# A delta-rule attention feeding an MLP on one core: small identity products at the head of TensorE's program, and another order of the prologue

## The chip, the cores and the metric

The kernel runs on one core of a Trainium2 chip. The metric is the device time of one execution in microseconds (us). A core has engines that run side by side, each with its own program, in order: TensorE (PE in the profile, its weight loads PEld), VectorE (DVE), ScalarE (ACT), GpSimd (POOL) and SyncE (SP), which here only issues DMA transfers. An instruction that needs another engine's result waits on a semaphore, and everything behind it on its engine waits with it.

## The reference

Four batches, eight heads, 768 tokens, head dimension 48. For each head the state is a 48 x 48 matrix that is updated token by token; the outputs, laid out as 3072 tokens x 384, go through an MLP with hard-swish.

```python
k_n = k / (np.linalg.norm(k, axis=-1, keepdims=True) + 1e-06)
for t in range(S):
    y[:, :, t] = np.einsum('bhd,bhde->bhe', q[:, :, t], state)
    v_old = np.einsum('bhde,bhd->bhe', state, kt)
    state = state + bt[:, :, :, None] * np.einsum('bhd,bhe->bhde', kt, vt - v_old)
...
h = x @ w_in                       # 3072 x 384 by 384 x 2048
g = h * np.clip(h + 3.0, 0.0, 6.0) / 6.0
return (g @ w_out).astype(np.float32)
```

All inputs and outputs are float32.

## The kernel before

**The tiling.** Tokens are taken in 24 steps (t = 0 to 23) of 32 tokens; four batches of 32 tokens fill the 128 partitions. Inside a step the token-by-token recurrence is turned into products of 32 x 32 matrices per head and batch, with the inverse of a triangular matrix; between steps the 48 x 48 states are carried. Two steps make one block of 256 tokens for the MLP.

**One step of attention** has these parts, each a generator that gives its work out in pieces:

- `norms` (L397 to L434): the key norms, a square on ScalarE (L407), a sum and four small rows on VectorE (L413 to L431), a root on ScalarE (L417).
- `prep` (L505): normalised keys `kb` on POOL (L510), transposes of keys and queries on TensorE (pt, L524), their copies KQ on ScalarE (L532), the scores sc on TensorE (L547, 32 small products for a step), and two masked copies on VectorE (L558), called L and LB.
- `mask` (L475) and `scaled` (L494) on POOL: the masks with beta (L486) that L558 multiplies by, and keys times beta (L498). The mask of step t waits for the L of step t - 2.
- the inverse. Step 0 has its own (`product`, L569: pi at L596). Steps 1 to 4 form a group: `halves_of` (L715) turns their four L into one tile A on VectorE (L469), eliminates with 14 pairs of rows `pr` and `A` (L730, L735), and turns it back into X (L473). For each of these steps `join` (L666) then makes the whole inverse from two halves: a transpose on VectorE (L694), 32 products pi1 (L684), a sum and a transpose (L698, L702), 32 products pi2, and a copy into X on ScalarE (L710).
- `chain` (L787): products with the state, ks (L806); R on VectorE (L901, L909); pz = X by R (L827) and its copy on ScalarE, also called R (L927); the state's update su on TensorE (L938) and on VectorE (L956); and `output`: y (L843, L819), py (L827), yt (L873) and its copy xT (L877), which is the MLP's input.

**The MLP.** `up` (L982) makes h for a chunk of 128 features as three products ph (L994), then on ScalarE a relu (L1001) and on VectorE g (L1004). `down` (L1153) multiplies by w_out. Later blocks use versions with fewer products (L1059, L1207). Before a weight is used it is converted: weights arrive as 16 pieces of 768 KB that SP loads (L331) into `spare` or into parts of w_out, four rows on ScalarE make a scale (`scales`, L356), and three rows on VectorE (`convert`: L378, L383, L389) make the piece. There are two scale tiles, so the first scale row of piece i waits for L389 of piece i - 2, and `up` of two chunks waits for one piece of w_in.

**The order.** The first 5 steps or so are not scheduled by rule. A string, `ORDER` (L22 to L41), gives one word for each piece of work, and the engines' programs stand in that order: `k`, `q`, `v`, `w` a load; `n`, `p`, `m`, `b`, `x`, `h`, `y` a piece of `norms`, `prep`, `mask`, `scaled`, `product`/`join`, `chain`, `output` of the step that is named; `i1` a piece of the inverse of steps 1 to 4; `a` one scale row, `c` one conversion row, `s` and `z` settings on POOL and VectorE; `ua`, `ra`, `ga` one chunk of `up` for the first half block, its relu and its g. `x2*3` is the word three times. After the string a loop (L1469) runs step by step, with the work spread by budgets.

PSUM tiles come from rings: four buffers for transposes, pi, pz, py, yt and ph, and two pairs of banks for sc, ks and su. A new tile takes the buffer whose reader was issued first.

Of the kernel before, what the change touches and what calls it, by code (L numbers as in the profile page):

```python
# [22 lines left out]
k*2 B*3 k*2 n0 k*2 z B s*2 n0*6 k*2 q*2 n1 q n1 q w k p0 z*3 k n1*2 k*2 n1*2 z p0*2 s k p0*3 a k a  # L23
m0 a n2 m1 p0 x0*2 w q x0 n1 x0*3 c*2 n2 a k s p1*2 a s*2 k q s*2 x0 n2 k*2 c x0 n2 x0 w q a*4 q p1
n2 k*2 a x0 m2 p1 c*2 p1 n2*3 b1 q b0 s p1 x0 q w x0 n2 q*2 c*3 x0 n4 k p1 k p2*2 x0*2 a*2 c a*2 q*3
a*2 w v p3*2 q x0 q n4 p2*2 c p2 v c n4*2 a*3 z v n4 c a m3 v c p2 n4*2 q p2 k c b2 h0 c h0 w a*2 h0
p4*2 a*2 m4 p3 q*4 h0 q k w p4*2 c*5 v*2 p3 k p3*3 k*2 p4*2 v*2 p4 m6 k a w a w i1*3 k i1*7 a i1*2 a
i1*2 v i1*2 k b3 k y0 c y0*3 ua*2 ra*2 i1*3 w v ga v a*3 i1*2 ua i1 h1 i1 q w ua ra ua i1 ra*2 ga i1
k ua a*2 ra ga i1 ga ua ra ua ra i1 ga i1*4 ua ga n5 x1*2 k x1 c a ra v a*2 ga x2 k*2 ga*2 ua*2 x1
ra*2 x1*2 ua h1*2 n5 k ga c ra ga*2 h1 c y1*2 ua ra w ga ua ra x2 n5 ga y1*2 ua ra ga h1 v*3 n5*2 k  # L30
y1*2 ua a ra x2 ub*2 a n5 rb*2 h1 x3 ga c*2 v W a h2 y2 gb ub rb gb x2 gb ub*2 n5*2 b4 rb n5 x2*2 h2
gb rb gb m5 a n5*2 y2 ub rb gb v c q*2 v q*5 n5 ub n5 rb gb h2 c h2 q ub y2 h2 y2 rb ub p5 b5 rb
gb*2 a*2 x3 p5 ub y2*2 k p5*2 h2 rb h3 p5 gb h3 ub*2 q rb gb rb gb ub a x3 p6 v c x4 x3 rb gb ub p7
rb gb y3 c*2 v c p7*2 y3 v p7*2 b6 x3 q x3 ub p6 h3 a p6 c p5*2 rb gb k m7 w p6 h3 u p6 k*2 q*3 a*2
y3 a p6 c y3 v y3*2 u n9 v k q a c a c*2 u*2 ru gu w k a*2 c a*2 x4 c*2 ru p7 a gu k u a*2 p7 p6 m8
u*3 a k u*2 k h3 w ru*2 a*2 gu*2 x4 c*2 x4 k c*2 a p8 k a*2 u ru k h3 u*2 h4 ru a b8 gu k gu y4 p8*3
u h4 k*2 c q k*9 q u p8*2 x4 k ru k*2 gu k c n9 q u q*2 p8 k*2 b7 n9*2 i2 u x4 q i2*2 q ub ru gu u
rb gb i2*2 h4*2 u*2 i2 ru i2*6 y4 i2 gu i2*7 u i2 ru gu i2 u*3 ru i2*4 gu ru i2*2 v i2 c gu u*3 a u
ru c i2 u*2 i2 gu i2*3 q i2*5 y4 h4 n9 i2 e*2 n9*2 i2*4 q i2 y4 e n9 u ru i2*3 u i2 ru*2 gu h4 u n9
i2*2 u i2 e i2*6 y4 u k n9*3 u gu i2 y4 n9 i2 p9 q i2*2 gu  # L40
"""  # L41


# [1 line left out]
def kernel(  # L45
# [21 lines left out]
    nc = tc.nc  # L67
    B, H, S, D = q.shape
    DM, FF = moe_w_in.shape
    C, DP = 32, 64  # L70
# [11 lines left out]
    G0 = 1  # L82
# [12 lines left out]
    def rows(b):  # L95
        return slice(C * b, C * b + C)
# [4 lines left out]
    def group(t):  # L101
        return (0, t) if t < G0 else ((t - G0) // GS + 1, (t - G0) % GS)
# [34 lines left out]
    def needs(*what):  # L137
        assert past.issuperset(what), (what, set(what) - past)
# [70 lines left out]
    ident = const.tile([128, 128], FP32, name="ident")  # L209
# [284 lines left out]
    def scaled(t):  # L494
# [7 lines left out]
        past.add(("bkb", t))  # L502
        yield

    def prep(t, whole=True):  # L505

        g, i = group(t)
# [9 lines left out]
        for j, src in enumerate((kb, qb)):  # L517
            if j == 1:
                needs(("q", t))
                past.add(("qT", t))  # L520
            ring("pm", NPM, ("pt", t, j))
            pt = psM.tile([128, NP, P], FP32, name="pt", tag=slot["pm"])
            for p in range(NP):
                nc.tensor.transpose(  # L524
                    pt[:, p, :], src[:, 2 * p : 2 * p + 2].rearrange("p e w -> p (e w)"), ident[:]
                )
            yield 1
            if j == 0:
                ring("KQ", NKQ, ("KQ", t))
                KQ = work.tile([128, NP * B // 2, 4, C], FP32, name="KQ", bufs=NKQ)  # L530
            read(("pt", t, j))
            nc.scalar.activation(  # L532
                out=KQ[:, :, 0:4:3, :] if j == 0 else KQ[:, :, 1:3, :],
                in_=pt[:].rearrange("q p (x y c) -> q (p x) y c", y=2, c=C), func=ACTF.Copy,
            )
            if whole and j == 0:
                drain(mask(t))
            yield
# [3 lines left out]
        for p in range(NP):  # L542
            for b in range(B):
                for e in range(2):
# [4 lines left out]
                        lhsT=kq[:, 3 if b % 2 else 0, :],  # L549
                        rhs=kq[:, 3:1:-1, :] if b % 2 else kq[:, 0:2, :],  # L550
                        start=True, stop=True,
# [114 lines left out]
    def join(t):  # L666
# [11 lines left out]
        def times(name, m, k):  # L678
            ring("pm", NPM, (name, t))
            ps = psM.tile([P, H, HC], FP32, name="pi", tag=slot["pm"])  # L680
            for h in range(H):
                for b in range(B):
                    r = slice(C * b, C * b + k)
                    nc.tensor.matmul(  # L684
                        ps[rows(b), h, :], lhsT=m[r, h, :], rhs=LT[r, h, HC:C],
                        start=True, stop=True, skip_group_check=True,
                        tile_position=(C * b, C * b),
                    )
            return ps
# [6 lines left out]
        ps = times("pi1", T, HC)  # L696
# [10 lines left out]
        ps = times("pi2", T2, C)  # L707
# [694 lines left out]
    def early_norms(t):  # L1402
# [7 lines left out]
        a=scales(), c=rest, w=pieces(), q=queries(), v=values(), B=betas(), k=keys(), z=settings(), s=more_settings(),  # L1410
        ua=up(0, 0), ub=up(0, 1), u=mlp_units(),
# [40 lines left out]
    with tc.manual_schedule():  # L1452
        for word in ORDER.split():
            word, _, n = word.partition("*")
# [14 lines left out]
        for t in range(LS, N):  # L1469
            g, i = group(t)  # L1470
# [94 lines left out]
```

## Time and profile before

| | |
|---|---|
| runs | 661.84, 663.70, 664.44 us; median 663.7 |
| the profiled execution | 662.06 us, span 660.3 |
| TensorE busy | 632.5 us, 96% of the span, 11640 matmul passes |
| VectorE busy | 499.2 us, 76% |
| ScalarE busy | 282.3 us, 43% |
| POOL busy | 225.1 us, 34% |
| chain that ended last | TensorE 91%, VectorE 3%, DMA 2% |
| DMA | 33.28 MB, of it instructions 1.49 MB in 91 packets (q8) |

In the rows of a timeline the first two numbers are the start from the span's beginning and the duration in us, then engine, line, operation, output tile from input tiles, shape and count; a bracket tells how long the engine stood idle before and what released it. A float32 matmul of the program can be two passes on TensorE, so 32 small products stand as x64. Spans are modelled at a matmul's end. "PEclk" is the granted TensorE clock as a share of full speed.

The profile shows two stretches: a prologue of some 61 us, where TensorE is busy in parts, and then 599 us in which it is busy throughout.

### The profile page before, as it was taken

To read this page: it belongs to the slowest core of one execution; us is meant where nothing else is said; L and a number is where in the kernel's file an instruction comes from. 1 tells how busy PE (TensorE), PEld (TensorE's weight loads), DVE (VectorE), ACT (ScalarE), POOL (GpSimd) and SP (SyncE) were. 2 spreads that over 40 slices of the span, in tenths; PEclk is the share of its full clock that TensorE was granted. 3 is DMA by queue.
4 is the path that set the end of the run, shared out by engine and by line. 5 is a ranking of instruction groups with operands and counts; after the bars stand their busy time and mean duration, and the time that the engine had idled before them with its cause. 6 is when DMAs were issued, how large, how long until landed. Compare 5 with 4: busy or idle time off the path is not lost.

```text
span 660.3 us, 26640 instructions
## 1 busy us (share of the span) xinstructions
PE 632.5 (96%) x11640; PEld 569.2 (86%) x11640; DVE 499.2 (76%) x1170; ACT 282.3 (43%) x548; POOL 225.1 (34%) x352
## 2 busy tenths in 40 slices
PE   2768999999999999999999999999999999999997
PEld 2658987776689989999999999999999999999997
DVE  5899877798657988758988848979658998456354
ACT  5887689332243154154154244244244144153250
POOL 6531022003661353553254354164051242331430
PEclk9998999999999999999999999999999999999999
DMA  7888346202040030041030030020020020000000
GB/s 174 204 198 235 77 102 164 51 25 43 9 87 18 3 74 3 3 90 22 3 74 3 2 74 3 2 63 2 3 50 2 3 49 3 23 18 2 26 1 24
DMA packets 88692, 33.28 MB, mean 50 GB/s; under 512 B 80224, under 2 KB 83424, under 8 KB 88576
## 3 DMA queue, kind: packets, MB, share of 16 engines
q1 hardware_dynamic: 88224, 31.29, 20.8%
q8 instruction: 91, 1.49, 0.9%
q10 hardware_dynamic: 352, 0.30, 0.2%
q14 instruction: 25, 0.20, 0.1%
HBM read 26.84 MB, written 4.72 MB: 48 GB/s over the span
## 4 chain that ended last, share of the span: by engine, by line
PE 91%; DVE 3%; DMA 2%; SPq 1%; ACT 1%; issue 1%; DVEq 0%
PE po L1226 28%; PE ph L1066 27%; PE ph L994 9%; PE po L1162 6%; PE ks L806 4%; PE su L938 3%; PE pt L524 3%; PE pz L827 3%; PE py L827 3%; PE sc L547 2%; PE yt L873 1%; DMA spare<-in_moe_w_in_dram 1%; PE pi L684 1%; DMA w_out<-in_moe_w_in_dram 1%; SPq L168 1%
## 5 line engine op out<-in xcount | busy, mean ns | idle before, releaser
L1066 PE MATMUL ph<-xT,w_in 128*128 128x128 f32 (+1 forms) x720 | 156.8, 321 | 0.0
L1030 POOL TENSOR_TENSOR g<-g 128x256 f32<-128x256 f32 (+1 forms) x144 | 88.6, 616 | 104.7 <-ACT g L1080 99.1
L1066 PEld LDWEIGHTS ph<-xT,w_in 128*128 128x128 f32 x720 | 116.8, 191 | 6.7
L1226 PE MATMUL po<-w_out,g 128*128 128x192 f32 x640 | 110.6, 326 | 0.0
L1226 PEld LDWEIGHTS po<-w_out,g 128*128 128x128 f32 x640 | 104.6, 190 | 0.5
L1080 ACT ACTIVATE g<-ph 128x512 f32<-128x512 f32 x72 | 43.1, 598 | 105.1 <-PE ph L1066 105.1
L1226 PE MATMUL po<-spare,g 128*128 128x192 f32 x480 | 86.7, 332 | 0.0
L1226 PEld LDWEIGHTS po<-spare,g 128*128 128x128 f32 x480 | 77.2, 190 | 1.8
L994 PE MATMUL ph<-xT,w_in 128*128 128x128 f32 (+1 forms) x384 | 72.0, 338 | 0.6 <-ACT xT L877 0.6
L1236 POOL TENSOR_TENSOR o<-o,u 128x192 f32<-128x192 f32 x18 | 13.3, 739 | 163.8 <-ACT o L1233 86.6
L994 PEld LDWEIGHTS ph<-xT,w_in 128*128 128x128 f32 x384 | 59.6, 195 | 7.7 <-ACT xT L877 0.8
L1093 DVE TENSOR_TENSOR g<-ph,g 128x256 f32<-128x256 f32 x72 | 30.2, 419 | 46.8 <-PE ph L1066 33.5
L759 DVE TENSOR_TENSOR pr<-A 128x30 f32<-128x30 f32 (+9 forms) x150 | 57.3, 382 | 3.3
L1212 DVE TENSOR_TENSOR g<-g 128x512 f32<-128x512 f32 x80 | 56.1, 722 | 3.5 <-PE po L1226 3.5
L1113 DVE SCALAR_TENSOR_TENSOR g<-o,g 128x512 f32<-128x512 f32 x72 | 52.6, 730 | 7.8 <-ACT o L1110 7.7
L764 DVE TENSOR_TENSOR A<-A,pr 128x30 f32<-128x30 f32 (+9 forms) x150 | 55.1, 367 | 3.3
L1110 ACT ACTIVATE o<-g,halves 128x512 f32<-128x512 f32 x72 | 52.2, 725 | 11.3 <-DVE g L1113 8.4
L1066 PE MATMUL ph<-beta_tok,sums_in 128*128 128x128 f32 x288 | 55.9, 275 | 0.0
L356 ACT ACTIVATE spare<-spare,places 128x768 uint16<-128x768 uint16 (+1 forms) x56 | 52.8, 947 | 3.2 <-DMA kf<-in_k_dram 1.6
L1233 ACT ACTIVATE o<-po 128x192 f32<-128x192 f32 x40 | 13.3, 332 | 82.7 <-PE po L1226 79.2
L510 POOL TENSOR_TENSOR kb<-kf,inv 128x384 f32<-128x384 f32 x24 | 21.7, 907 | 75.5 <-issue 43.1
L1162 PE MATMUL po<-w_out,g 128*128 128x384 f32 x128 | 45.4, 490 | 0.0
(141 smaller groups left out, 1019.1 us busy)
## 6 DMA issues: line engine op xcount, KB each, us to landing
kf<-in_k_dram SPq DMA_DIRECT2D x96, 48.0 KB, 2.6
qb<-in_q_dram SPq DMA_DIRECT2D x96, 48.0 KB, 2.4
vf<-in_v_dram SPq DMA_DIRECT2D x96, 48.0 KB, 2.1
out_dram<-o SPq DMA_DIRECT2D x90, 48.0 KB, 1.6
spare<-in_moe_w_in_dram SPq DMA_DIRECT2D x4, 768.0 KB, 6.6
w_out<-in_moe_w_in_dram SPq DMA_DIRECT2D x4, 768.0 KB, 6.1
w_out<-in_moe_w_out_dram SPq DMA_DIRECT2D x4, 768.0 KB, 5.8
spare<-in_moe_w_out_dram SPq DMA_DIRECT2D x4, 768.0 KB, 5.2
```

Source lines behind the costliest of these rows:

```text
L356: nc.scalar.activation(out=z, in_=z if n else d.bitcast(I16)[:, :, :, 3], func=func, bias=places[:, n : n + 1], scale=scale,)
L759: nc.vector.tensor_tensor(out=pv, in0=A[:, j + 1 :, j].unsqueeze(2).to_broadcast([n, w, j]), in1=A[:, j, 0:j].unsqueeze(1).to_broadcast([n ...
L764: nc.vector.tensor_tensor(out=A[:, j + 1 :, 0:j], in0=A[:, j + 1 :, 0:j], in1=pv, op=ALU.subtract)
L994: nc.tensor.matmul(ph[:, cols], lhsT=w_in[:, s, f * 128 : (f + 1) * 128], rhs=xT[:, s, cols], start=(s == 0), stop=(s == NKT - 1),)
L1030: nc.gpsimd.tensor_tensor(out=out, in0=a, in1=b, op=op)
L1066: nc.tensor.matmul(ph[:, n], lhsT=w, rhs=x, start=start, stop=stop, skip_group_check=True)
L1080: nc.scalar.activation(out=gt, in_=ph[:], func=ACTF.Copy)
L1110: nc.scalar.activation(out=r, in_=g, func=ACTF.Relu, bias=half, scale=1.0 / 6.0)
L1113: nc.vector.scalar_tensor_tensor(out=g, in0=r, scalar=1.0, in1=g, op0=ALU.min, op1=ALU.mult)
L1162: nc.tensor.matmul(pos[c][:], lhsT=gs[blk, f // 2][:, f % 2, c * P : (c + 1) * P], rhs=w_out[:, f, :], start=(f == 0), stop=(f == NFC - 1),)
L1212: nc.vector.tensor_tensor(out=A(f, *out, 4), in0=A(f, *a, 4), in1=A(f, *b, 4), op=op)
L1226: nc.tensor.matmul(ps[n][:], lhsT=A(f - f % 2, *a)[:, f % 2], rhs=b[:, f], start=(f == 0), stop=(f == HF - 1),)
```

## The change

Two things.

1. A new function `small_ones` issues small products of the identity with itself (a 16 x 32 block by a 16 x 16 block, in turn on the four groups of 32 partitions). 58 stand at the head of TensorE's program, into the PSUM tile of step 0's first transposes, which then overwrite it. 6 more stand ahead of the 32 products pi1 of the first join (step 1), into that tile. Their results are never read.
2. Some five lines of `ORDER` are another permutation of the same work. On TensorE, the transposes and scores of steps 2, 3 and 4 now stand ahead of step 0's state update su (before, only step 2's scores did), all but the scores of step 4 also ahead of step 0's pz; two more chunks of `up` stand ahead of the first join, and one in place of two between its pi1 and pi2. On VectorE, the L and LB rows of steps 2 to 4 move up, and so does A, ahead of step 0's state rows (L956); of the conversions, four pieces rather than six are finished before A, and six rather than seven before the inverse is turned back (L473). The settings of `parity` move from before A to inside the elimination, and ten g rows rather than five stand before L473. On ScalarE, the KQ copies of steps 2 to 4 come before step 0's copy R, with 18 scale rows ahead of that copy rather than 20; 30 scale rows rather than 36 stand ahead of the first join's copy (L710), and the other six stand between it and step 1's copy R (L927). One w_in load moves behind two loads of q. POOL's order is the same. From step 1's py on the order is the same on every engine.

```diff
@@ ORDER
-a*2 w v p3*2 q x0 q n4 p2*2 c p2 v c n4*2 a*3 z v n4 c a m3 v c p2 n4*2 q p2 k c b2 h0 c h0 w a*2 h0
-p4*2 a*2 m4 p3 q*4 h0 q k w p4*2 c*5 v*2 p3 k p3*3 k*2 p4*2 v*2 p4 m6 k a w a w i1*3 k i1*7 a i1*2 a
-i1*2 v i1*2 k b3 k y0 c y0*3 ua*2 ra*2 i1*3 w v ga v a*3 i1*2 ua i1 h1 i1 q w ua ra ua i1 ra*2 ga i1
-k ua a*2 ra ga i1 ga ua ra ua ra i1 ga i1*4 ua ga n5 x1*2 k x1 c a ra v a*2 ga x2 k*2 ga*2 ua*2 x1
-ra*2 x1*2 ua h1*2 n5 k ga c ra ga*2 h1 c y1*2 ua ra w ga ua ra x2 n5 ga y1*2 ua ra ga h1 v*3 n5*2 k
+a*2 w v p3*2 m3 b2 q n4 x0 q p2*2 n4 c p3 v*2 p3 n4 p2 n4*3 p4 c p4 p3 p2 p4 v q*3 w c p3 a p2 m4 c
+k p4 p3 p4 h0 a c p4 q*3 k w h0 p4 i1 a v*2 k*3 h0 a y0 v*2 h0 c y0 k w y0 a y0 w m6 i1*3 ua a k
+i1*3 ra ua z i1*2 a ga ra ua v i1*2 a ga ra h1 k b3 k i1*3 ga c*2 ua ra w ua ra i1*3 ga a c v ua ra
+ga i1*3 ua ra ga a v i1*3 ua ra ga i1*3 ua ra ga a q w i1*2 ua ra ga a k i1*2 ua ra ga a i1 x1*2 x2
+x1 n5 c k x1 ua ra a h1 ga x1*2 c v k*2 a h1 c a*2 c a*3 n5 k c ga h1 c y1*2 ua ra w ga ua ra x2 n5
...
+    def small_ones(ps, n):
+        for i in range(n):
+            b = i % B
+            nc.tensor.matmul(
+                ps[rows(b), 0, 0 : C // 2], lhsT=ident[C * b : C * b + C // 2, 0:C],
+                rhs=ident[C * b : C * b + C // 2, 0 : C // 2],
+                start=True, stop=True, skip_group_check=True, tile_position=(C * b, C * b),
+            )
+
+    LEAD, TRAIL = 58, 64 - 58
...
+            if (t, j) == (0, 0):
+                small_ones(pt, LEAD)
             for p in range(NP):
                 nc.tensor.transpose(
...
+            if (t, name) == (G0, "pi1"):
+                small_ones(ps, TRAIL)
             for h in range(H):
```

## The prediction

> **What bounds the kernel now.** First the page's busy tenths, to find where TensorE is not full. The 40 slices are 16.5 us each:
>
> ```profile
> PE   2768999999999999999999999999999999999997
> DVE  5899877798657988758988848979658998456354
> ACT  5887689332243154154154244244244144153250
> PEclk9998999999999999999999999999999999999999
> ```
>
> Only the first four slices fall short, with VectorE (DVE) near full there. A table of stretches gives it in us (PE, PEld, DVE, ACT, POOL busy, then TensorE's granted clock, DMA share, GB/s):
>
> ```profile
> 34.00:48.00 14.00, 9.63 (x398) 8.17 (x396) 12.63 (x32) 13.05 (x18) 3.47 (x4) 1.00 0.82 195
> 48.00:61.20 13.20, 9.80 (x121) 9.05 (x121) 12.41 (x40) 10.11 (x19) 2.20 (x5) 0.87 0.95 269
> 61.20:67.40 6.20, 6.16 (x226) 5.68 (x227) 6.06 (x16) 4.86 (x11) 2.15 (x4) 1.00 0.49 146
> 67.40:660.30 592.90, 589.52 (x10362) 531.74 (x10361) 444.68 (x1028) 231.70 (x469) 198.76 (x290) 1.00 0.15 33
> ```
>
> From 61.2 on TensorE has work all the time: a microsecond lost or won before then is one at the end, and nothing else counts. Up to 61.2 VectorE sets the pace. The timeline has the places (start, duration, what):
>
> ```profile
> 35.99 2.88 ACT L356 ACTIVATE spare<-spare,places 128x768 uint16<-128x768 uint16 x3
> 38.77 0.47 ACT L927 ACTIVATE R<-pz 128x384 f32<-128x384 f32 x1
> 39.29 1.27 PE L938 MATMUL su<-R,sums_in 32*64 32x48 f32 x61 [1.75 <-ACT R L927]
> ...
> 47.70 1.93 DVE L469 STREAM_TRANSPOSE A<-L 128x1024 f32<-128x1024 f32 x1
> ...
> 51.05 3.55 PE L994 MATMUL ph<-xT,w_in 128*128 128x128 f32 x18 [0.58 <-ACT xT L877]
> ...
> 58.71 2.00 DVE L473 STREAM_TRANSPOSE X<-A 128x1024 f32<-128x1024 f32 x1
> ...
> 61.24 0.72 PE L684 MATMUL pi<-X,sums_in 16*32 16x16 f32 x64 [0.94 <-DVE sums_in L694]
> ...
> 64.22 0.28 ACT L710 ACTIVATE X<-pi 128x128 f32<-128x128 f32 x1
> ...
> 65.94 0.49 ACT L927 ACTIVATE R<-pz 128x384 f32<-128x384 f32 x1 [0.51 <-PE pz L827]
> ...
> 67.37 0.88 PE L827 MATMUL py<-R,LB 32*32 32x48 f32 x64
> ```
>
> The recursion of steps one to four starts on VectorE at 47.70 (A), is back at 60.71 (X), goes through the first join (61.24), and step one's output product py runs at 67.37. From py on the changed program has the same order on every engine, so the sum is: when does py start now.
>
> **Products.** The 58 stand ahead of the first transpose, which starts at 8.08. The identity is there at 1.9. A product is two passes (the 32 of a score group show as x64), 116 passes; 64 passes of pi at 13.65 took 1.08, so 2.0 us, over by 4: cost 0, covered by the wait for the first keys, 2.0 without it. The six are 0.2 us in the wait for the join. Instruction fetch: 23,280 PE and PEld instructions in 91 packets are 256 a packet; 64 products make one packet, so what follows the join keeps its place in a packet and only the prologue moves. A packet takes 0.9% x 16 x 660.3 / 91 = 1.04 us. TensorE shows no wait that a packet would explain after 61.2, and before it VectorE is the pace: cost 0, bounds 0 to 1.04.
>
> **Scores earlier: A starts about 6.1 sooner.** Step two's L ended at 38.33; it is no earlier now, because its scores stand behind the transposes of step three's keys: VectorE's root steps end near 34.5 (they follow the L378 of 33.21), keys 0.83 on POOL, four transposes 0.85, 32 scores 1.18, L written by 38.2. Step four's masks wait for that L on POOL. The two rows for two masks differ:
>
> ```profile
> 38.71 2.62 POOL L486 TENSOR_TENSOR sums_in<-beta_tok,mask 128x256 f32<-128x256 f32 x2
> 47.93 1.19 POOL L486 TENSOR_TENSOR sums_in<-beta_tok,mask 128x256 f32<-128x256 f32 x2 [6.61 <-DVE LB L558]
> ```
>
> I take 2.62, since VectorE works through that time as it did at 38.71: 40.9, plus the L and LB products 0.75: A at 41.6 (40.2 with 1.19).
>
> **What slides in between A and X.** A to X was 13.0 us with one w_in product (L389) and five g products (L1004). Now there are also, in VectorE's order: two state updates 1.01 (row of 71.42), one more L389 0.87, L378 and L383 0.55 + 0.96, the nine parity writes 0.44, five more g products at 0.14 to 0.20, 0.8. Together 4.6. X is back at 41.6 + 13.0 + 4.6 = 59.2, 1.5 sooner and not 6.
>
> **After X the change gives it back.** X to the end of R's second half (L909) is 3.55 as before (60.71 to 64.26). Then VectorE still has a g product, L383 and L389 of the seventh weight piece, 0.27 + 0.96 + 0.95 with gaps 2.2: 64.95. ScalarE (ACT) has six weight scalings (L356) between the copy of X (L710) and the copy of R (L927), where there was only one g row before. Four of them belong to the ninth piece and wait for that seventh L389, since the scale tiles are two. Four scalings, copy, start on TensorE is in the rows: 34.96 to 39.29, 4.33. So py is at 64.95 + 0.06 + 4.33 = 69.35. ScalarE alone says the same: X copied by 62.9 (one row of three up-products stands between the join's halves now), 6 x 0.97, 0.49, 0.1: 69.3. Against 67.37 that is **+2.0**. Queued behind L927 on ScalarE are y's even part and the g rows, on TensorE everything from py on. Bounds: +0.6 with the cheap masks, +3.4 if A is 1.4 late (step four's KQ copy behind one scaling more).
>
> SP: one w_in load moves behind two q and ahead of one k, 0.45 an issue, 0.9 late; issued near 33.8 it lands by 40.4 (6.6 for such a load), and its first reader, a scaling on ScalarE, comes after 44: cost 0. POOL keeps its order.
>
> **Clock.** TensorE's busy time in stretches of 3.4 us, with its clock:
>
> ```profile
> 48.70:52.10 3.40, 1.60 (x11) 0.96 1.04 326
> 52.10:55.50 3.40, 3.40 (x56) 0.54 1.03 277
> 58.90:62.30 3.40, 2.46 (x80) 1.00 0.78 215
> ```
>
> A stretch with 1.60 busy was followed by one at half clock; with 2.46 it wasn't. At half clock 18 passes took 3.55, at full clock 2.21 (chain of waits, 86.09): 1.34 a stretch. Before, VectorE's pace hid that. Now TensorE has nothing to do from about 66.2 (the triples ahead of py) to 69.35, so it is likely slow just when it becomes the bound. About half of its time after py is up-products: 0.7 a stretch, one or two stretches, 0 if the borders fall well: I take +0.9, bounds 0 to 2.8 (four).
> The Trainium skill (TensorE: Matmul & The Clock Gate, "Why this matters for your kernels") says to leave no TensorE gap over about 3 us, since a window of some 3.4 us without work halves the clock. The trace agrees, with the stretch of 0.54. By the page's halving alone one window of full work would lose 1.7 us (an estimate from that page), and the sum would be +3.7 in place of +2.9.
>
> **Sum.** +2.0 + 0.9 = +2.9 us. The profiled execution took 662.06 (span 660.3 and 1.8 around it), so 665.0; it lies 1.6 under the median 663.7 of the runs (661.84 to 664.44). On the median: **666.6**.
>
> **Rivals.**
> *Not slower: A starts by 39.6.* Step two's scores were done by 36.1 before and L was held by VectorE's queue. If keys of step three are early, L ends at 36.9, the masks cost 1.19 and A starts at 38.9; X is back at 56.5 and py at 66.65, -0.7, without a long gap: 663.0. It decides below 39.6 (41.6 - 2.0). Against it: the root steps for step three stand behind two weight rows on VectorE. 0.12.
> *The clock costs more than it hides.* Four stretches at half clock, +2.8: 663.7 + 4.8 = 668.5. For it: the triples at 45 to 56 are thinner too. 0.15.
> *The recursion doesn't start as early as it says*, A at 43.0, or one instruction packet late on the path: +3.4 (+3.0) and 0.9 of clock: 668.0. For it: six groups of 128 small instructions (scores, pz, su, py) now follow one another, three packets, with the DMA share at 0.8 to 1.1. 0.13.
> The forecast case, +2.0 for py with some clock, has 0.60.
>
> **Numbers.** 0.5% (3.3 us) is about what a measurement can tell from no change. The forecast case runs from +0.6 to +4.4, some 0.22 of its 0.60 above 3.3. Slower by over 0.5%: 0.22 + 0.13 + 0.10 = 0.45; faster: 0.05, the far end of the first rival; within: 0.50. Range: from 662.5 (the first rival's 663.0, less half a us of run spread) to 669.8 (668.5 and the rest of the packet's price); about 0.08 lies under it and 0.12 above.
>
> **What would show it.** In the profile after: the 58 products over before 5 us; L469 near 41.6; L473 ending near 59.2 with state rows and two L389 ahead of it; at the join six L356 rows between L710 and L927, and L927 near 68.8; py near 69.3 with a TensorE wait of about 3 us on ACT R; granted clock near half within 5 us of py; from there the same rows as before, shifted alike. It is wrong if L927 follows L710 closely, if L473 ends before 57.2, or if TensorE's full stretch after py is not the old one's length.

## The result, and the profile after

The changed kernel takes 673.65 us (median of 5, 672.69 to 675.33) against 662.23 for the kernel before (median of 5, 661.84 to 664.44): ratio 1.0162, 95% interval 1.014 to 1.0184. It is 1.6% slower, some 11 us, where 2.9 were forecast. The profiled execution took 674.05, its span is 672.2; the span before was 660.3.

The page's busy tenths of the kernel after; the slices are 16.8 us each:

```profile
PE   3667899999999999999999999999999999999997
DVE  4868776799748888858988848989748988557253
PEclk9967599999999999999999999999999999999999
```

TensorE was at 9 from the fifth slice on and is now from the sixth; its clock is down in slices three to five. For the kernel before the profile has no record of the clock ahead of 44.98, so its 9 and its 1.00 up to there are filled in, not measured. Its pz, 64 passes, took 1.50 us by this row of its timeline, as py does in the kernel after at half clock (77.21 below); at full clock py took 0.88 (67.37 before):

```profile
36.03 1.50 PE L827 MATMUL pz<-vf,X 32*32 32x48 f32 x64
```

A slow clock ahead of A is therefore not new. What is new is half clock from 43.64 to 57.30, where the kernel before had it from 51.80 to 55.22, and from 67.54 to 81.19, where it had none. The stretches of the kernel after (us, then PE, PEld, DVE, ACT, POOL busy with instructions, granted clock, DMA share, GB/s):

```profile
34.00:48.00 14.00, 8.46 (x298) 6.85 (x300) 7.95 (x16) 6.95 (x10) 3.33 (x5) 0.62 0.78 192
48.00:68.20 20.20, 16.12 (x334) 14.53 (x325) 16.79 (x58) 12.39 (x23) 1.98 (x5) 0.75 0.62 174
68.20:78.90 10.70, 8.70 (x213) 7.77 (x212) 8.59 (x18) 8.59 (x14) 2.86 (x4) 0.50 0.36 100
78.90:672.20 593.30, 589.60 (x10297) 531.35 (x10297) 443.28 (x1025) 230.31 (x467) 201.43 (x290) 1.00 0.15 33
```

Up to A VectorE, which set the pace before (12.63 of 14.00 us busy), is now idle nearly half the time (7.95): something else is late. The timeline of the kernel after says what (a releaser "issue" means that TensorE waited for nothing that the profile shows):

```profile
38.10 2.05 PE L560 MATMUL sc<-KQ 64*32 64x64 f32 x128
...
40.72 0.87 PE L842 MATMUL pz<-vf,X 32*32 32x48 f32 x60
...
45.23 0.37 PE L842 MATMUL pz<-vf,X 32*32 32x48 f32 x4 [3.64 <-issue]
...
45.53 1.18 PE L560 MATMUL sc<-KQ 64*32 64x64 f32 x64
...
47.49 1.95 DVE L469 STREAM_TRANSPOSE A<-L 128x1024 f32<-128x1024 f32 x1
...
52.82 4.21 PE L1009 MATMUL ph<-xT,w_in 128*128 128x128 f32 x18 [0.58 <-ACT xT L892]
...
64.82 1.94 DVE L473 STREAM_TRANSPOSE X<-A 128x1024 f32<-128x1024 f32 x1
...
67.30 0.92 PE L699 MATMUL pi<-X,sums_in 16*32 16x16 f32 x64 [2.88 <-DVE sums_in L709]
...
73.91 2.87 ACT L356 ACTIVATE spare<-spare,places 128x768 uint16<-128x768 uint16 x3
...
76.69 0.47 ACT L942 ACTIVATE R<-pz 128x384 f32<-128x384 f32 x1
...
77.21 1.50 PE L842 MATMUL py<-R,LB 32*32 32x48 f32 x64 [1.38 <-ACT R L942]
```

Inside one group of products, pz, after 60 of its 64 passes, TensorE stands for 3.64 us. The releaser is "issue": no semaphore, no data. The scores behind it (sc) are A's last input, so A starts at 47.49, where it was forecast at 41.6 and stood at 47.70 before. The scores did go ahead of the state update; the time did not come with them. The first 18 passes of ph then take 4.21 us, at half clock.

The path splits into four parts (us; the last number of the profile is py to the end of the span):

| | A starts | A to X back | X to py | py to the end | span |
|---|---|---|---|---|---|
| before | 47.70 | 13.01 | 6.66 | 592.9 | 660.3 |
| forecast | 41.6 | 17.6 | 10.15 | +0.9 | +2.9 |
| after | 47.49 | 19.27 | 10.45 | 595.0 | 672.2 |

Against the forecast A is 5.9 late, the recursion 1.7 longer, the way from X to py 0.3, and the rest 1.2: together 9.1, all of the miss between the two profiled executions (9.0). The theories for it:

- **Position.** The products move the bounds between TensorE's instruction packets, and one now falls badly.
- **Order.** So many small instructions in a row need packets faster than they come, wherever the bounds lie.
- **Products.** They cost by themselves.
- **Clock.** Half clock costs more than forecast.

### The profile page after: what moved, and what is told of

The parts are those of the page before. It is cut to its first block, busy times and chain, and to the rows that moved or that the text cites. A ratio compares the mean times of both kernels' runs of the same rounds, so it can differ in the third digit from the quotient of the medians.

```text
span 672.2 us, 26895 instructions
## 1 busy us (share of the span) xinstructions
PE 640.8 (95%) x11768; PEld 575.4 (86%) x11768; DVE 499.2 (74%) x1170; ACT 280.9 (42%) x548; POOL 227.9 (34%) x352
## 4 chain that ended last, share of the span: by engine, by line
PE 90%; DMA 3%; SPq 2%; DVE 2%; issue 1%; ACT 0%; POOL 0%; DVEq 0%
PE po L1241 28%; PE ph L1081 27%; PE ph L1009 9%; PE po L1177 6%; PE ks L821 4%; PE py L842 3%; PE su L953 3%; PE pz L842 3%; PE pt L537 3%; PE sc L560 3%; DMA w_out<-in_moe_w_in_dram 2%; PE yt L888 1%; SPq L168 1%; DMA kf<-in_k_dram 1%; PE pi L699 1%
## 5 line engine op out<-in xcount | busy, mean ns | idle before, releaser
L1081 PE MATMUL ph<-xT,w_in 128*128 128x128 f32 (+1 forms) x720 | 156.8, 321 | 0.0
L1081 PEld LDWEIGHTS ph<-xT,w_in 128*128 128x128 f32 x720 | 116.8, 191 | 6.7
L1009 PE MATMUL ph<-xT,w_in 128*128 128x128 f32 (+1 forms) x384 | 75.7, 350 | 1.0 <-ACT xT L892 0.6
L1251 POOL TENSOR_TENSOR o<-o,u 128x192 f32<-128x192 f32 x18 | 16.3, 906 | 160.9 <-ACT o L1248 86.7
L1009 PEld LDWEIGHTS ph<-xT,w_in 128*128 128x128 f32 x384 | 62.5, 206 | 9.2 <-ACT xT L892 1.0
```

The costliest lines, as they stand in the source:

```text
L1009: nc.tensor.matmul(ph[:, cols], lhsT=w_in[:, s, f * 128 : (f + 1) * 128], rhs=xT[:, s, cols], start=(s == 0), stop=(s == NKT - 1),)
L1081: nc.tensor.matmul(ph[:, n], lhsT=w, rhs=x, start=start, stop=stop, skip_group_check=True)
```

## The experiments

### The two parts of the change, alone

Order alone, `order_alone`:

```diff
-    LEAD, TRAIL = 58, 64 - 58
+    LEAD, TRAIL = 0, 0
```

> All 64 small products left out, which take no part in the result; the new order stays. Three theories of the 10 us that the change cost. Position: TensorE's instructions come in packets of 256, and 58 products of 4 instructions each move the bounds between packets by 232; in the changed kernel a late packet stopped TensorE for 3.64 us inside pz (41.59 to 45.23), and without the products that stop falls at another place, or nowhere, with A (L469) near 41.6 as forecast and the time near 667 (662.23 plus the 2.4 that the longer path from X to py costs, plus 1 to 3 of half clock). Order: the new order asks for small instructions faster than packets arrive, wherever their bounds lie; then a stop of 3 us or more stays before A, A starts after 45, and the time is 671 to 675. Products: the order costs nothing and the time is within 1 us of 662.2.

Measured: 671.64, ratio 1.0138 (1.011 to 1.0166). The stop and A are just under what Order theory said (3 us, 45): 2.87 us, and A at 44.97.

```profile
38.80 1.00 PE L842 MATMUL pz<-vf,X 32*32 32x48 f32 x48
42.67 0.41 PE L842 MATMUL pz<-vf,X 32*32 32x48 f32 x16 [2.87 <-issue]
```

Products alone are the string `ORDER` of before in the file after:

> The order of the kernel before, with the 58 small products ahead of the first transposes and six ahead of the first join. Position: the bounds between packets move by 232 instructions under the old order, so that the stop of 0.75 us before su (40.56) moves by nearly one packet, back to where it was less 24 instructions, and the time changes by 1 us or less, unless the new place is a bad one, when it is up to 4 us more. Order: within 0.7 us of 662.2. Products: near 673.

Measured: 664.78, ratio 1.0033 (1.0018 to 1.0047). The order has nearly all of the loss: without a product it still stops in pz, after pass 48, for 2.87 us. "Position" as the whole cause falls here. The products cost 2.8 us of their own by the medians under the old order, where nothing was forecast; under the new order, by the ratios, 1.6, with intervals that overlap. Where that is lost shows early: the second group of pi (32x64) starts at 18.00 in this run (before: 16.41), at 16.7 to 18.0 in the seven profiled kernels with 58 at the head, at 16.0 to 17.1 in the nine with 26 or none. What starts late ahead of it waits for a load. ScalarE's square of the second keys (L407) starts at 7.15 to 7.70 in the eight profiled kernels with 58 or more at the head and at 6.39 to 6.99 in the ten others; the eight alone move an instruction packet between 4.03 and 6.04, while those keys are on their way, and in the others the first one moves at 13.54 or later. So it is the packet that the 58 products use up, more than their passes, that goes with the loss; that it holds up the keys is argued, for no run moves a packet there without products. A follows at 49.40 (47.70), and X to py takes 1.06 longer, with a stop of 0.86 in pz at 68.09.

### Where the products stand

`LEAD, TRAIL = 0, 64` and `26, 64 - 26` under the new order:

> The new order with none of the small products at the head and all 64 ahead of the first join, so that up to the join the packets lie as with no products at all. Position: up to the join the trace is that of the order alone (the same stop or none, the same start of A), and behind it the packets lie as in the changed kernel; the 64 products take about 2 us in the wait of the first join for VectorE's row sums (2.88 us in the changed kernel) and cost nothing. Time within 1 us of the order alone. If the two differ by more, the products at the join or the packets behind it have a price of their own. Order: 671 to 675 for both.

> The new order with 26 products at the head and 38 ahead of the first join: up to the join the bounds between packets lie 128 instructions, half a packet, from where the changed kernel has them. Position: the stop of 3.64 us inside pz lies elsewhere, 128 instructions on (within the fourth chunk's scores sc, at A's last input) or about as many back (before pz, in sc of the third step), and the time differs from 673.65 by more than 1 us in one direction or the other. Order: the stop stays within pz and sc, as long as before, and the time is within 1 us of 673.65.

Measured: 671.21 (1.0107 to 1.0169) and 675.13 (1.0151 to 1.0223). The 64 at the join cost nothing under this order, as expected. The stop moves as instructions are counted: with none at the head it is at pass 48 of pz both times, as in the order alone; with 26 it is at pass 59 of sc and again at pass 58 of py. It never goes away. Its length is not fixed by position: 2.87 and 1.16 us at the same instruction. Nor is it fixed by the program. Three kernels of the sections below (wide products at the join, g sums later, scalings behind) give TensorE the same instructions up to A as the changed kernel, and all four stop behind pass 60 of pz, the changed kernel for 3.64 us:

```profile
44.20 0.37 PE L852 MATMUL pz<-vf,X 32*32 32x48 f32 x4 [0.59 <-issue]
42.05 0.28 PE L842 MATMUL pz<-vf,X 32*32 32x48 f32 x4 [0.81 <-issue]
43.27 0.27 PE L842 MATMUL pz<-vf,X 32*32 32x48 f32 x4 [1.14 <-issue]
```

Their A starts at 46.46 (behind three more stops, of 1.14, 1.53 and 0.58), 43.89 and 45.12. So bounds decide where TensorE stops; for how long differs from one execution to the next, and the profiled 3.64 is the longest of the four.

### How fast instructions come

The order of before with `LEAD, TRAIL = 320, 0`: small products and nothing else to wait for.

> The order of the kernel before with 320 small products, 1280 instructions or five packets, at TensorE's head and none at the join, to measure how fast small instructions can be supplied. Supply theory: TensorE runs out between packets; the products come in bursts of about 128 passes with a stop between them of 1 to 3 us, each ending 1.2 to 1.5 us after an instruction packet, and the 640 passes need 14 to 18 us. Rival, the chip brings instructions as fast as small products use them: no stop, 640 passes at 1.08 us for 64 in 11 us or less, and TensorE's stops in the other runs come from something else. Either way the first transposes start later than 8.08.

Measured: its one execution took 677.01. The timeline of that run:

```profile
1.95 3.18 PE L508 MATMUL pt<-ident 16*32 16x16 f32 x223 [1.95 <-POOL ident masks.py:199]
6.86 1.90 PE L508 MATMUL pt<-ident 16*32 16x16 f32 x128 [1.73 <-issue]
10.59 1.90 PE L508 MATMUL pt<-ident 16*32 16x16 f32 x128 [1.83 <-issue]
16.24 1.90 PE L508 MATMUL pt<-ident 16*32 16x16 f32 x128 [3.75 <-issue]
21.06 0.63 PE L508 MATMUL pt<-ident 16*32 16x16 f32 x33 [2.92 <-issue]
```

Behind the first burst they are bursts of exactly 128 passes, each a weight load and a product: 256 instructions, one packet. The 640 passes take 19.7 us, not 11. The trace has the packets on the instruction queue, and so the whole turn from one packet's first instruction to the next one's:

```
run, stop               first of packet   next packet moves    its first    turn
many small, 6.86        3.22              4.03 to 5.47         6.86         3.64
many small, 10.59       6.86              7.97 to 9.17         10.59        3.73
many small, 16.24       10.59             13.50 to 14.68       16.24        5.65
many small, 21.06       16.24             18.19 to 19.53       21.06        4.83
changed kernel, pz      38.98             42.74 to 43.78       45.23        6.26
order alone, pz         36.49             40.22 to 41.34       42.67        6.18
all at the join, pz     36.85             38.36 to 39.99       41.32        4.47
26 at the head, py      43.63             46.01 to 47.20       48.62        4.99
```

(First of packet: the pass 128 passes ahead of the stop, or the one behind the stop before.) This is what the forecast missed. In these rows the next packet starts to move 0.8 to 3.8 us after the first instruction of the one before, as if only one were fetched ahead; it moves for 1.0 to 1.6 us; 1.3 to 1.6 us later its first instruction runs. A turn takes 3.6 to 6.3 us, and 256 small instructions take 1.9 here (the clock has no record ahead of 41.31 in this run). In these rows TensorE stops where a packet holds less work and waiting than the turn of the next. What makes a turn 3.6 us or 6.3 no run shows. With the DMA share at 0.5 (4 to 12 us) the turns were 3.6 and 3.7, at 1.13 (12 to 16) 5.65, at 0.91 (16 to 20) 4.83.

The Trainium skill (Runtime: NRT & Kernel Launch, "Instruction fetch mechanics") has blocks of 256 instructions, the next fetched while the current one executes, at a cost that is mostly hidden. The traces agree on the 256 and on one ahead; for small products they disagree on hidden, by the 1.73 to 3.75 us above.

From the start of sc for steps two and three to the end of A's last scores lie 260 passes, 520 instructions, two packets with nothing else to wait for. In the twelve profiled kernels of this order A started at 43.26 to 47.49. The forecast's 41.6 had no packet in it. Taking the stops over half a us off one for one (an estimate), A would start at 41.1 to 42.6 in the six of them with 26 products or none at the head and at 42.2 to 44.0 in the six with 58: near the forecast, plus a us or so that goes with the products. That leaves little of A's delay for another cause.

### Is it a load, or the number of instructions?

A w_in load moved behind eight k and v loads (not ten, as the expectation has it). It is the one issued at 38.47, which the change left in its place among the loads; the one that the change moved is issued at 35.41. In `ORDER`, `q*3 k w h0` becomes `q*3 k h0`, and `k w y0` becomes `k w*2 y0`.

> The changed kernel with one w_in load (768 KB, issued on SP at 38.47) moved behind the ten k and v loads that follow, so that it is issued near 45. Contention theory: TensorE's packet at 42.74 came late because the DMA engines were full (share 1.09 to 1.15 from 38 to 44); with that load gone the share there falls below 0.9, the stop in pz (3.64 us) shrinks to 1.5 or less, A starts 2 us sooner or more, and the time is 1.5 to 3 us less than the changed kernel's. Rival: the packet is asked for too late, whatever else moves; the stop stays over 2 us or moves to the next group, and the time is within 1 us of 673.65.

Measured: 672.02 (1.0097 to 1.015). The stop is 2.11 us and the turn 4.36; but kernels with the load in place also had turns of 4.2 to 4.5 there, and the intervals overlap. Not settled; longer turns with fuller DMA engines show only in the four turns of the run of many small products.

Fewer instructions for step zero, as many columns:

```diff
-            for h in range(H):
+            for h in range(H if t else 1):
+                n = D if t else D * H
...
-                        ps[rows(place(b)), D * h : D * h + D],
-                        lhsT=m(h)[rows(b)], rhs=z[rows(b), D * at(h) : D * at(h) + D],
+                        ps[rows(place(b)), D * h : D * h + n],
+                        lhsT=m(h)[rows(b)], rhs=z[rows(b), D * at(h) : D * at(h) + n],
```

and su likewise; once under the new order, once under the old without products.

> The changed kernel with fewer instructions for step zero alone: pz and py with one product over all eight heads' columns where there were eight, su with one over four where there were four, so 80 products and 320 instructions less and as many columns written (the values of step zero, and of all that follows from it, are then not the reference's). The pz, sc, su, py groups that followed each other now hold 324 instructions in place of 640. Supply theory: the stop in pz goes or moves out of the way of A; A starts by 43.0 (47.49 in the changed kernel), TensorE is not half slow for all of 43 to 57, X is back 4 to 6 us sooner and the time is 667 to 670. Rival, A's late start has another cause (POOL's keys, ScalarE's KQ copies at 40.83 and 45.65): A within 1.5 us of 47.49 and the time at 672 or more.

> The kernel before, its order and no small products, with the same thinned step zero (80 products and 320 instructions less, values not the reference's): the control for the run with the new order. In this order TensorE waits for ScalarE's R between pz and su and has 0.75 us of stop in su; so supply costs it little, and the time is 660.5 to 662.5. The difference between the two thinned kernels is what the order costs without most of the supply's part: 5 to 8 us if supply was worth 3 or more of the 11, still 10 to 11 if it was worth nothing.

Measured: 671.44 (1.0118 to 1.0203) and 666.4 (1.004 to 1.0088). Both expectations missed. Under the new order, timeline:

```profile
39.73 0.85 PE L843 MATMUL pz<-vf,X 32*32 32x384 f32 x8
40.50 0.74 PE L560 MATMUL sc<-KQ 64*32 64x64 f32 x51
44.28 0.34 PE L560 MATMUL sc<-KQ 64*32 64x64 f32 x13 [3.03 <-issue]
```

The 112 instructions saved in pz only pushed the bound 51 passes into sc; the turn was 6.25 all the same, and A started at 45.44, between the two theories' numbers. The control is the surprise: its py of step 1 starts 1.1 us late, but it ends 5.7 late. The timeline of the control, 250 us in, where the kernel before has no such stop:

```profile
249.72 0.86 PE L843 MATMUL py<-R,LB 32*32 32x48 f32 x59
252.42 0.28 PE L843 MATMUL py<-R,LB 32*32 32x48 f32 x5 [1.84 <-issue]
...
254.59 1.92 PE L1083 MATMUL ph<-xT,w_in 128*128 128x256 f32 x4
```

A packet's bound lies in py, behind 64 passes of su: 1.84 us of stop, and then products at half the rate (1.92, elsewhere 1.03). From the ninth y to the eleventh the delay grows from 2.4 to 5.9. Taking 320 instructions away made the kernel slower.

### The scalings between X and py

In `ORDER`, after the third `a h1`: `c a*2 c a*3 n5 k c ga h1 c y1*2 ua ra w ga ua ra x2 n5 ga y1*2` becomes `c a c n5 k c ga h1 y1*2 ua ra a*2 c w ga ua ra a x2 n5 ga a y1*2`.

> The changed kernel with the four scalings (L356) of the ninth weight piece moved on ScalarE from ahead of the copy of R (L942) to behind it, between the next rows. Forecast's step: the six scalings in a row cost py 2 to 4 us; with two left, R's copy follows pz by about 73.0 in the changed kernel's times, py is at 73.5 in place of 77.21, and the time falls by 2.5 to 3.8 us, to 670 to 671. Rival: what is moved is paid behind py (the eighth and ninth pieces are needed soon after, and TensorE waits for their up-products there), and the time stays within 1 us of 673.65.

Measured: 671.64 (1.0092 to 1.0166), the profiled span 669.8. The timeline:

```profile
71.16 0.47 ACT L942 ACTIVATE R<-pz 128x384 f32<-128x384 f32 x1
...
71.17 2.93 PE L1009 MATMUL ph<-xT,w_in 128*128 128x128 f32 x12
...
74.03 1.50 PE L842 MATMUL py<-R,LB 32*32 32x48 f32 x64
```

R's copy now follows pz at once, as the forecast's step says, and X to py is 9.11 in place of 10.45. It is not the 6.66 of before: what was hidden under the scalings comes out, TensorE's own rows at half clock (ph x12 in 2.93). By the medians the gain is 2.0 against the changed kernel; the intervals overlap. Between the profiled executions it is 2.4, but A alone starts 2.4 sooner there (45.12), ahead of the edit; the 1.35 won between X and py is given back from A to X (0.5) and behind py (0.8).

### The clock

Three wide products in place of three small ones at the join:

```diff
-                small_ones(ps, TRAIL)
+                small_ones(ps, TRAIL - WIDE)
+                for _ in range(WIDE):
+                    nc.tensor.matmul(
+                        bank[:].rearrange("p (n c) -> p n c", c=P), lhsT=ident[:],
+                        rhs=ident[:].unsqueeze(1).to_broadcast([P, 4, P]),
+                        start=True, stop=True, skip_group_check=True,
+                    )
```

> The changed kernel with three of its six products ahead of the first join made wide: the full 128x128 identity against 512 columns in place of 16x16, some 1 us each at full clock, the same number of instructions. They fill TensorE's wait for VectorE's row sums (64.4 to 67.3 in the changed kernel). They take no part in the result. Clock theory: the half clock from 67.54 to 81.19 came from that wait; it is gone, the first join's products and all behind it run at full clock, py to the end shrinks from 595.0 to near 593 and the time is 1.5 to 2.5 us less than the changed kernel's (671 to 672.3). R's copy itself waits for ScalarE's six scalings, which know no clock, so py moves by under 0.7. Rival: the clock behind the join is set by the gap ahead of py, not by the one ahead of the join; then the half clock stays and the time is 673 to 674.5.

Measured: 674.5 (1.015 to 1.0193). The join ran at full clock (pi 0.73 where it was 0.92, half clock only from 70.0 to 80.2), and nothing was gained: the scalings set py. Next, the g sums: in `ORDER`, three `ga` moved behind `c*2`.

> The changed kernel with the first three g sums (L1019) on VectorE behind the L378 and L383 that follow them in the recursion, nothing else moved. In the changed kernel VectorE waits 1.32, 0.52 and 0.19 us for them, since the first 18 passes of ph took 4.21 us at half clock (2.21 at full). If half clock costs the recursion those waits, X is back 1.3 to 2.0 us sooner, A to X is 17.3 to 18.0 in place of 19.27, and the time is 1.3 to 2 us less than 673.65. Rival: VectorE only waits elsewhere (for the fourth sum, or at the join), and the time is within 0.7 us.

Measured: 671.96 (1.0122 to 1.0187); A to X 19.72, no shorter. The rival's mechanism holds: VectorE waits 0.61 and 0.98 us for the next sums, which come from ph products just as slow. The time is not within the rival's 0.7 us, but the 3.0 us between the profiled spans are A's start, 3.6 sooner (43.89) and ahead of the edit.

All repairs at once (no small products, load later, four scalings behind R, sums later):

> The new order without the 64 small products, with the w_in load later, four scalings behind R's copy and the three g sums later, all at once: what is left of the order's price when each found cost is taken off. If they add up (products 2, load 1.6, scalings 2, sums 1.5 of the 11.4): 666 to 667.5. If they share one cause, the late packets, and each only buys what another already bought: 668.5 to 671. Faster than the kernel before (below 662) would take the first join 4 us earlier than any of these costs explains.

Measured: 668.59 (1.007 to 1.0114), at the lower edge of the second expectation, costs that share a cause. That speaks for it without showing it, for the interval, 667.0 to 669.9 us, reaches into the first. Its stretches of 3.41 us, on the borders of its clock:

```profile
47.25:50.67 3.42, 2.27 (x67) 1.67 (x63) 3.16 (x14) 1.88 (x4) 0.00 (x0) 0.50 0.91 304
50.67:54.08 3.41, 3.38 (x16) 3.38 (x17) 3.08 (x15) 2.41 (x5) 0.00 (x0) 0.50 1.08 291
54.08:57.50 3.42, 3.42 (x85) 3.25 (x85) 2.33 (x9) 1.68 (x5) 0.00 (x0) 1.00 0.89 226
...
60.90:64.32 3.42, 0.32 (x3) 0.13 (x2) 3.35 (x10) 2.90 (x6) 0.00 (x0) 1.00 0.65 170
64.32:67.73 3.41, 3.40 (x133) 3.13 (x134) 2.54 (x8) 0.73 (x2) 1.38 (x3) 0.50 0.02 5
67.73:71.15 3.42, 2.79 (x86) 2.49 (x78) 3.35 (x6) 3.23 (x6) 1.48 (x2) 0.50 0.26 71
71.15:74.56 3.41, 3.41 (x74) 3.07 (x74) 3.35 (x9) 2.76 (x5) 0.00 (x0) 0.50 0.78 232
```

Read each row's busy time (second number) against the clock of the row below it. At half clock 2.27 and 2.79 us of 3.41 kept the next stretch at half, and so did 3.40 us of mostly small passes (the join's, x133). What brought full clock back was 3.38 us of large products (ph, x16) and 3.41 of ph and py (the last row was followed by full clock). The same count over the first 130 us of all eighteen profiles, in stretches on each one's borders: at full clock 38 stretches with under 1.69 us busy were all followed by half clock, and of 323 with over 2.07 all but one by full clock. At half clock none of 66 with under 2.73 was followed by full clock, and 40 of 45 with over 2.98 were. The five that were not hold 104 to 128 passes of the join (tiles 16x16 and 32x16), and so does the one at full clock. So a clock that is down is harder to raise than one that is up is to keep, and the join's passes seem to count for less than their time. Small passes as such don't: in the run of the order alone 165 passes, nearly all of 64x64 and 32x48, filled the stretch from 36.05 to 39.46 and full clock followed. The price of the clock can be had by filling with large products; first the join's wait, in the kernel with all repairs, then also the recursion:

```diff
+            if t == 0:
+                nc.tensor.matmul(pt[:, 0, :], lhsT=ident[:], rhs=ident[:], start=True, stop=True)
             for s in range(NKT):
                 nc.tensor.transpose(pt[:, s, :], y[:, s * 128 : (s + 1) * 128], ident[:])
```

and the same ahead of the first ph.

> The run with all repairs (668.59) and three wide identity products ahead of the first join (128x128 against 512 columns, which take no part in the result), in TensorE's wait for VectorE there. In the changed kernel wide products there bought nothing (674.5), because py waited for ScalarE's scalings; with four of these behind R, TensorE's own rows stand between X and py, at half clock (pi 1.05, ph 1.65, pi 1.05, pz 1.50, ph 2.93 us; at full clock 0.73, 0.94, 0.73, 0.88, 1.60). Clock theory: X to py shrinks from 9.14 to 6.5 to 7.5 and the time to 665.5 to 667. Rival: the clock falls again ahead of py, as before, and the time is within 0.7 us of 668.6.

> The same with one more 128-column identity product ahead of step zero's transposes of y and one ahead of its first up-products, in TensorE's waits of 0.61 and 0.58 us there (no part in the result). With all repairs the stretch of 3.42 us from 47.25 held 2.27 us of TensorE's work and the next went at half clock (18 passes of ph in 3.87 us), while stretches of 3.38 were followed by full clock. Clock theory: the stretch fills to 3.2, the next goes at full clock, VectorE's waits for the g sums (0.31 and 0.71) end, A to X falls from 19.3 to 18.0 to 18.5 and the time is 0.7 to 1.5 us under the run without them. Rival: the stretch stays under the mark, the products only delay ph by 0.3 to 0.9, and the time is the same or 0.5 more.

Measured: 672.6 (1.0111 to 1.0162) and 671.04 (1.0095 to 1.0146), by the medians both slower than the run without them (the intervals touch). Part by part the clock theory holds: X to py fell from 9.14 to 8.16 (1.0 us, less than expected) and A to X, with full clock from 50.9 on, from 19.65 to 18.07. So half clock costs the recursion some 1.6 us. But py to the end grew from 594.3 to 598.7 and 597.8: the 12 instructions more at the join moved every later bound, and one fell into the transposes of y behind py and sc (in the second run, with 20 more, one fell into sc: 1.71 us at 104.00). Timeline of the first of the two:

```profile
102.97 0.44 PE L898 MATMUL yt<-ident,y 128*128 128x128 f32 x2
105.33 0.48 PE L898 MATMUL yt<-ident,y 128*128 128x128 f32 x1 [1.92 <-issue]
105.60 2.77 PE L1187 MATMUL po<-w_out,g 128*128 128x384 f32 x4
```

Again a stop, and a stretch at half clock behind it (105.4 to 108.8). The fifth y is 9.1 us late where the fourth was 5.3.

### Position, under the old order

`LEAD, TRAIL = 0, 48` and `0, 64` with the old `ORDER`:

> The order of the kernel before, nothing else changed, with 48 small products ahead of the first join and none at the head (no part in the result). They are 192 instructions, three quarters of a packet, and take 0.7 to 1 us where TensorE waits 0.94. In the thinned kernel in this order (320 instructions less, so the same places within packets from the join on) TensorE stopped for 1.84 us in the py of step 8 near 250 us, 59 passes into it, behind 64 passes of su, and a stretch at half clock followed: 3.5 us. Position theory: the same stop comes here, near 250, at the same pass, and the time is 665 to 667.5. Order or products theory: no such stop, and the time is within 1 us of 662.3.

> The same with 64 products, 256 instructions, one packet, so that all that follows the join stands in its packet where the kernel before has it. Position theory: no stop near 250; the time is 662 to 663.3, at most the 0.3 to 0.5 us by which 64 products may overrun a wait of 0.94 us. If it is slower than that by 1 us or more, the products themselves cost, or the packet more does. Beside the run with 58 at the head and six at the join (664.78) it shows whether the head is where those lost their 2.8 us.

Measured: 668.6 (1.0045 to 1.0096) and 669.64 (1.0079 to 1.0117). By the medians the losses are 5.2 and 6.2 us. The first is more than position theory said, and not at its place: there is no stop near 250. There are stops of 0.98 (pi, 65.58), 0.61 (ph, 69.14), 0.98 (py, 85.49) and 1.13 (py, 177.02); the one in ph is at the same pass as a stop of 0.21 in the control. How long each is varies with the turn. The second refutes the expectation outright, and shows why in its timeline:

```profile
62.46 1.23 PE L508 MATMUL pi<-ident 16*32 16x16 f32 x126 [0.64 <-DVE g L1019]
...
63.56 0.61 PE L699 MATMUL pi<-X,sums_in 16*32 16x16 f32 x53
66.48 0.26 PE L699 MATMUL pi<-X,sums_in 16*32 16x16 f32 x9 [2.31 <-issue]
66.67 2.32 PE L1009 MATMUL ph<-xT,w_in 128*128 128x128 f32 x12
```

Idle products and the join's passes behind them run through a packet in 1.06 us (62.93 to 63.99); the next is not there, TensorE stops for 2.31 us, and ph x12 then runs mostly at half clock (2.32; at full 1.60). The products overrun the wait by 0.75 (the join's input was ready at 62.77, its product started at 63.52); the packet they spend costs more. (Under the new order, where that wait was 2.88 us, the same 64 cost nothing.) What follows in each packet is as before, and after py this kernel loses only 0.7 us more.

## Why the prediction was wrong

**Products, "cost 0, bounds 0 to 1.04".** This is the step that failed, and in it the part on instruction fetch. It took a packet's price to be the 1.04 us for which it moves; the price is a turn of 3.6 to 6.3, less what TensorE has to do in it, and the new order stops for it ahead of A in all twelve of its profiled kernels. It also looked for a wait "that a packet would explain" in the trace of before, where 0.75 us in su was the only one over half a us: too little to show what a faster sequence would meet. The third rival had the right mechanism ("six groups of 128 small instructions ... now follow one another, three packets"), at one packet and +3.0, and got 0.13. The products themselves cost 2.8 us under the old order, and in the profile of that run half of the loss, 1.7, is at the head, where the forecast had them covered.

**Scores earlier, A at 41.6.** Wrong with it: 47.49, and 43.26 at best. 5.9 of the missing 9.1 us, of which 3.64 is the stop in pz. How much of it an execution meets is luck: the same instructions on TensorE also gave stops of 0.59 to 1.14 and A from 43.89.

**Between A and X, +4.6.** The rows that slid in are there; 6.3 measured. With TensorE at full clock from 50.9 on it took 18.07, in the unthinned kernels without that 19.3 to 20.2: most of the excess is half clock, through the g sums that VectorE works off in order.

**X to py.** Right: 10.45 against 10.15, with six scalings between L725 and L942. The last four start at 72.89, just behind the L389 that ends at 72.84, as forecast, and py follows at 77.21, 4.32 later (forecast 4.33). Under them lay a second cover that the forecast did not name: TensorE's rows at half clock, which kept 9.11 when the scalings were gone.

**SP load, cost 0.** Not tested: no run moves that load back, and the run with a load later moved the next one.

**Clock, +0.9, bounds 0 to 2.8.** Mis-sized. It was down from 43.64 to 57.30 and from 67.54 to 81.19, four stretches each time and not one or two. Half clock is worth about 1.6 in A to X, where the forecast had nothing, and up to 2.1 behind py, within its bounds; 3.7 together. The clock did fall behind the empty stretch ahead of the join, as the Trainium skill (TensorE: Matmul & The Clock Gate, "Why this matters for your kernels") has it: 0.54 us busy from 64.12 to 67.54. The traces go further than that: stretches with up to 2.06 us busy were followed by half clock too, so an idle window is not needed. The stretch by which the forecast let the trace agree was no idle one either (1.60 us busy; 1.30 on the clock's own borders). That the clock would stay down for four stretches the forecast had as a bound and as a rival (0.15) only.

**The sum.** +2.9 forecast; +11.9 between the profiled spans. Over the forecast 5.9 is A, 1.7 A to X, 0.3 X to py and 1.2 behind py. That the time rose, as forecast, comes from A to X and from X to py; that it rose by 11 and not by 3 comes most from A, where the forecast had instruction fetch at 0. No version tried beats the kernel before; 668.59, with all repairs, is the nearest of the new order.

## What to carry to other kernels

Count instructions, not only microseconds, before packing small products together: by the turns seen here 256 instructions need some 4 to 6 us of TensorE work and waiting to cover the next packet's, and waits that look wasteful may be that cover. An edit that adds or drops a few TensorE instructions moves every later packet's bound, so read the whole timeline for stops released by "issue", and compare variants by their parts, not by the total alone. A stop costs twice where it lets the clock fall, since half clock stayed here until a stretch was nearly full (2.73 us of 3.41 at least). And look at a stop in more than one execution before pricing it: the same one took 0.59 to 3.64 us.

## What the runs showed of the hardware that was not expected

- An instruction packet is asked for late: turns of 3.6 to 6.3 us between the first instructions of two packets, so that packets of 256 small instructions, 1.9 us of work each, did not follow each other without a stop.
- 320 instructions less (the control) cost 4.1 us by the medians, with a stop 250 us in that the kernel before has not; 12 and 20 more (the wide products) cost 4.0 and 2.5 by the medians, or 2.9 and 1.9 by the ratios to the kernel before beside each, with intervals that touch, although they shortened the parts that they were made for.
- At half clock a stretch of 3.41 us with TensorE busy for 3.40, mostly with the join's passes of 16x16 and 32x16, was followed by half clock again, where 3.41 us with 165 passes of mostly 64x64 and 32x48 brought full clock; at full clock over 2.07 us kept it in 322 of 323 stretches.
- An instruction packet that moved at 4 to 6 us went with keys that came 0.2 to 1.3 us later, in all eight kernels that had one there.
